# Gathered rows turned by DMA as fp16 halves, instead of by TensorE as fp32, in an attention and mixture-of-experts kernel

## The chip, the cores and the metric

The kernel runs on one core of one Trainium2 chip. The metric is the device time of one execution in microseconds (us); a run is timed several times and the median counts. A separate execution, recorded by the hardware profiler, gives the profile and the trace. Engines are named as in the profile: PE is TensorE's matmul, PEld its weight load, DVE VectorE, ACT ScalarE, POOL GpSimd, SP SyncE, and SPq the DMA queue that SP issues.

## The reference

Thresholded attention makes 4608 rows `x` of 512 numbers. Each row goes to one of 8 experts, which is a two-layer network with a ReLU, and comes back scaled by its gate.

```python
x = attn_out.transpose(0, 2, 1, 3).reshape(B * S, H * D)       # 4608 x 512
e_idx = np.argmax(x @ w_gate, axis=1)
for e in range(8):
    mask = e_idx == e
    h = np.maximum(x[mask] @ w1[e], 0.0)                       # 512 -> 1024
    out[mask] = gate_w[mask, None] * eom[mask, e, None] * (h @ w2[e])
```

## The kernel before

The first part, to about 464 us of the trace, is attention. Its rows are scattered by expert into a DRAM buffer `xs`. The second part runs the experts over **units**, blocks of rows of one expert that lie together in `xs`. There are 12, numbered 0 to 11, of 366, 424, 496, 420, 256, 512, 256, 504, 256, 396, 256 and 496 rows. The first two have a size and place fixed ahead, the third a fixed place; the rest are picked at run time (`choose`, a chain of small DVE operations). A unit of 256 rows is narrow (two tiles of 128 rows), the others are wide (four tiles, unit 0 three).

`Experts.run` walks the units in eight **columns** each (`f` = 0 to 7, 128 of the 1024 hidden features at a time). In a column PE runs `first(f)` (12 matmuls of f16 over all rows of the unit: the operands are split into a high and a low f16 part, `xh`, `xl`, `w1h`, `w1l`), ACT makes the ReLU `hr` and its high part `hh`, DVE the low part `hl`, and PE runs `second` of the column two back. In between the loop places other work: half a weight chunk split into f16 (`split_until`: ACT makes `w1h` or `w2h`, DVE `w1l` or `w2l`), the largest value of a later chunk (`look`), one step of the router (`advance`, `aside`), loads of weights (`load_next`, tile `r`) and of rows (`gather_next`, tiles `xg` wide and `xgn` narrow). The order on PE, DVE, ACT and POOL is the order of this code; SP's order is the framework's.

The rows arrive with a row on each partition. The matmuls want features on partitions, so each unit's rows are prepared while the unit before runs:

1. `level` hands out the pieces of `even`: the largest absolute value of each row (`most`, L933, two tiles at a time), a power of two from it (`xup`), then the rows scaled in place (`scale`: L943 on DVE, or L941 on ACT for units 1 to 4).
2. `prep` in columns 5 and 6 (6 and 7 of unit 1): PE turns the scaled fp32 rows against an identity into PSUM (`px`, L1260; L1397 in class `Turned`, the units of 424, 420 and 396 rows), ACT casts `xh` out of PSUM (L984), DVE subtracts for `xl` (L990).

Unit 0 does the same inside the attention's last steps. Class `Turned` also loads its rows in three DMAs so that its short tile comes first.

Of the kernel before, what the change touches and what calls it, by code (L numbers as in the profile page):

```python
# [430 lines left out]
class Router:  # L431
# [5 lines left out]
    def __init__(self, ctx, tc, ntok, E, DM, sizes, cut):  # L437
# [260 lines left out]
    def choose(self):  # L698
# [14 lines left out]
        for k, z in enumerate(self.SLOTS):  # L713
            yield
            read = z if z < self.TURNED else -(-z // P) * P
            V.scalar_tensor_tensor(key[:, 0:E], st[:, 1], float(read), st[:, 0], op0=ALU.is_ge, op1=ALU.mult)
            V.tensor_reduce(top, key, axis=AX.X, op=ALU.max)
            V.tensor_scalar(cand, key[:, 0:E], top, None, op0=ALU.is_equal)
            V.tensor_tensor(pick, st[:, 2:4], cand[:, None, :].broadcast_to([1, 2, E]), op=ALU.mult)
            yield  # L720
            V.tensor_reduce(got, pick, axis=AX.X, op=ALU.add)
            V.tensor_scalar(self.prows[:, 1, k : k + 1], got[:, 0:1], -1.0, dummy, op0=ALU.mult, op1=ALU.add)
            V.tensor_copy(self.prows[:, 0, k : k + 1], got[:, 1:2])
            V.scalar_tensor_tensor(
                st[:, 0:3], cand[:, None, :].broadcast_to([1, 3, E]), -float(z), st[:, 0:3], op0=ALU.mult, op1=ALU.add
            )
            self.tables.append(k)
# [69 lines left out]
class Experts:  # L797
# [28 lines left out]
    def open(self):  # L826
# [7 lines left out]
        ]  # L834
        self.xp = self.pool("ex", 2)
        self.fp = self.pool("ef", 1)
# [90 lines left out]

    def even(self, xg, other=False):
# [3 lines left out]
        def most(a, b):  # L932
# [5 lines left out]
        def scale(a, b):  # L938
            for t in range(a, b):
                if other:  # L940
                    self.nc.scalar.activation(xg[:, t, 0:DM], xg[:, t, 0:DM], AF.Copy, scale=up[:, t : t + 1])  # L941
                else:
                    V.tensor_scalar(xg[:, t, 0:DM], xg[:, t, 0:DM], up[:, t : t + 1], None, op0=ALU.mult)  # L943

        two = [(t, min(t + 2, n)) for t in range(0, n, 2)]
        return down, [lambda f=f, ab=ab: f(*ab) for f in (most, scale) for ab in two]

# [103 lines left out]

    def level(self, i, k):
        for n in sorted(self.since):
            if self.column - self.since[n] >= self.LOOK and (n < i + 3 or i > 3) or n == i + 1 and k >= -4:
                del self.since[n]
                self.pieces += [(n, x) for x in self.unit(n).even()]
        if i == 1 and k < -1:
            return
        self.pieces.sort(key=lambda x: x[0])
        due = sum(n == i + 1 for n, _ in self.pieces)  # L1060
        assert not due or k < 0
        count = max(int(self.unit(i).N > 2 * P), due + 1 + k if due else 0)
        for _ in range(min(count, len(self.pieces))):
            self.pieces.pop(0)[1]()

# [74 lines left out]
    def run(self):  # L1140
# [4 lines left out]
        for i in range(nun):  # L1145
            b, final = self.unit(i), i == nun - 1
            late = i == rt.early - 1
            for f in range(8):
# [25 lines left out]
                self.look(i, f)  # L1174
                self.level(i, k)
                for _ in range(1 if self.padded else 6 if rt.last else 3 if i or f else 0):
# [34 lines left out]
class Base:  # L1211
# [22 lines left out]
    def even(self):  # L1234
        self.down, pieces = self.ex.even(self.xg[:, 0 : self.nt], 0 < self.i < 5)
        return pieces

# [3 lines left out]

    def prep(self, k, later=None):
        ex, nc, rt, nt = self.ex, self.nc, self.ex.rt, self.nt
        if k == 1 and later is None:
            self.key()
        if k == 0:
            n = 512 if ex.units[0] is not self else nt * P
            self.xh = ex.xp.tile([P, 4, n], F16, name="xh")
            self.xl = ex.xp.tile([P, 4, n], F16, name="xl")
        chunks = 4 if nt == 2 else 2  # L1250
        if k * chunks >= 4:
            return
        pts = ex.px()
        hs = [slice(0, 64), slice(64, P)]
        for c in range(chunks):
            cs = slice((chunks * k + c) * P, (chunks * k + c + 1) * P)
# [4 lines left out]
        at = lambda x: x[:, chunks * k : chunks * k + chunks, 0 : nt * P].rearrange("p c (t h j) -> p h c t j", h=2, j=64)  # L1261

        def out():
            for h in range(2):
                pts[h] = pts[h][:, 0 : chunks * nt * 64].rearrange("p (c t j) -> p c t j", t=nt, j=64)
# [4 lines left out]
        if later is None:  # L1270
            out()
        else:
            later.append(out)

# [61 lines left out]
class Pair(Base):  # L1336
# [9 lines left out]
    def load(self, dst, r0, n):  # L1346
        rt = self.ex.rt
        src = rt.xs[bass.ds(self.row + r0, n), :]
        ins = self.nc.sync.dma_start(dst, src if n < P else src.rearrange("(t p) w -> p t w", p=P))
        rt.after(ins, [x for _, x in rt.tok])  # L1350
        rt.after(ins, rt.pads)

    def gather(self):
        self.xg = self.ex.rows_tile(self.nt)
        self.load(self.xg[:, 0 : self.nt], 0, self.nt * P)


# [18 lines left out]
class Turned(Pair):  # L1376
    def gather(self):
        xg = self.xg = self.ex.rows_tile(self.nt)
        m = self.nt - 1
        self.z = self.N - m * P  # L1380
        self.load(xg[:, 1 : self.nt], self.z, m * P)
        for pp in (slice(0, 64), slice(64, P)):
            self.load(xg[pp, 0], 0, 64)

    def prep(self, k):
        ex, nc, xg, m = self.ex, self.nc, self.xg, self.nt - 1
        if k == 1:
            self.key()
        if k == 0:
            self.xh, self.xl = (ex.xp.tile([P, 4, 512], F16, name=n) for n in ("xh", "xl"))  # L1390
        pts = ex.px()
        hs = [slice(0, 64), slice(64, P)]
        for b in range(2 * m + 1):
            for h in range(2):
                c, t = (b // m, 1 + b % m) if b < 2 * m else (h, 0)
                src = xg[hs[h], t, (2 * k + c) * P : (2 * k + c) * P + P]
                nc.tensor.transpose(pts[h][:, b * 64 : b * 64 + 64], src, ex.ident[hs[h], hs[h]])  # L1397
        at = lambda x: x[:, 2 * k : 2 * k + 2, self.z : self.N].rearrange("p c (t h j) -> p h c t j", h=2, j=64)
        parts = []
        for h, pt in enumerate(pts):  # L1400
            src = pt[:, 0 : 2 * m * 64].rearrange("p (c t j) -> p c t j", t=m, j=64)
            parts.append((at(self.xh)[:, h], at(self.xl)[:, h], src))
            one = (x[:, 2 * k + h, 0 : self.z] for x in (self.xh, self.xl))
            parts.append((*one, pt[:, 2 * m * 64 : 2 * m * 64 + self.z]))
        for hi, _, src in parts:
            ex.high(hi, src)
        for hi, lo, src in parts:
            ex.low(lo, src, hi)

    def second(self, f):  # L1410
# [20 lines left out]
    def flip(self, k):  # L1431
        ex, nc = self.ex, self.nc
        for i, pt in enumerate(ex.px()):
            t = 2 * k + i
            o = self.z + (t - 1) * P if t else 0
            for c in range(4):
                nc.tensor.transpose(pt[:, c * P : c * P + P], self.yt[:, c, o : o + P], ex.ident)
            ex.emit_out(pt, self.keys, t, slice(0, P if t else self.z))


class EarlyTurned(Turned):
# [7 lines left out]
    def load(self, dst, r0, n):  # L1449
        rt = self.ex.rt  # L1450
        src = rt.xs[self.row + r0 : self.row + r0 + n, :]
        ins = self.nc.sync.dma_start(dst, src if n < P else src.rearrange("(t p) w -> p t w", p=P))
        rt.read_early(ins)
# [72 lines left out]
def build(tc, qkv, tau, wg, w1, w2, out, shape):  # L1526
    nc = tc.nc
    with ExitStack() as ctx:
# [6 lines left out]
        with tc.manual_schedule(engines=ENGINES):  # L1535
            with ExitStack() as actx:
# [22 lines left out]

                def even():  # L1560
                    for piece in ex.unit(0).even():
                        piece()

                def begin():
# [16 lines left out]

                hooks[end] = even
                hooks[end + 1] = begin
# [55 lines left out]
```

## Time and profile before

| what | value |
|---|---|
| median of 3 timed runs | 888.5 us (887.51 to 890.45) |
| the profiled execution | 884.38 us, with a span of 882.7 us from first to last instruction |
| mean granted TensorE clock in the profiled execution | 0.998 of full speed |
| PE, DVE, ACT busy share of the span | 98%, 87%, 79% |

The span is what the trace shows; 1.7 us of the profiled execution's time lie around it. Time stamps below are in us from the span's start. A busy PE is an engine with matmuls in its pipeline, so the spacing of successive starts tells more than the busy share.

### The profile page before, as it was taken

How to read it: one execution, taken by the hardware profiler on the slowest of the kernel's cores; microseconds unless marked ns; L12 is line 12 of the kernel's file. 1: busy time of each engine (PE TensorE's matmuls, PEld its weight loads, DVE VectorE, ACT ScalarE, POOL GpSimd, SP SyncE). 2: the span in 40 equal slices, each digit the busy share in tenths (PEclk: the TensorE clock that was granted, in tenths of full speed). 3: DMA queues.
4: the chain of work that ended last, by engine and by line, in shares of the span. 5: the costliest groups of instructions: out<-in, count | busy, mean ns of one | idle time of the engine just before them, and what ended most of it. 6: DMA issues, size and time to landing. Idle time of an engine off the chain costs nothing. (4 is left out here: it accounts for less than half of the span.)

```text
span 882.7 us, 22316 instructions
## 1 busy us (share of the span) xinstructions
PE 866.9 (98%) x8271; PEld 524.6 (59%) x8271; DVE 764.8 (87%) x1839; ACT 700.6 (79%) x1349; POOL 407.5 (46%) x692
## 2 busy tenths in 40 slices
PE   8999999999999999999999999999999999999996
PEld 4666666666666666666665544455744655656643
DVE  6999999999999999999998877798797897886631
ACT  6999999998999998998987848776775775786731
POOL 4456656675867658676854650118210310310211
PEclk9999999999999999999999999999999999999999
DMA  6699995223332123313228688455573663550101
GB/s 196 192 273 301 338 308 185 89 92 100 125 104 74 60 80 124 125 45 112 80 84 272 217 257 286 138 159 169 194 233 97 215 214 97 191 190 2 38 24 46
DMA packets 74912, 135.16 MB, mean 153 GB/s; under 512 B 7295, under 2 KB 34175, under 8 KB 74802
## 3 DMA queue, kind: packets, MB, share of 16 engines
q1 hardware_dynamic: 68257, 114.80, 41.8%
q0 software_dynamic: 6544, 18.92, 5.6%
q8 instruction: 66, 1.08, 0.5%
q14 instruction: 45, 0.36, 0.1%
HBM read 95.26 MB, written 40.60 MB: 154 GB/s over the span
## 5 line engine op out<-in xcount | busy, mean ns | idle before, releaser
L177 ACT ACTIVATE p<-s,mn 128x576 f32<-128x576 f32 x288 | 216.0, 800 | 25.6 <-DVE s L159 25.4
L189 DVE SCALAR_TENSOR_TENSOR p<-s,thr,p 128x576 f32<-128x576 f32 x288 | 226.7, 824 | 0.3
L159 DVE TENSOR_SCALAR_CACHE_REDUCE s<-ps 128x576 f32<-128x576 f32 x288 | 206.2, 751 | 13.6 <-PE ps L145 11.4
L145 PE MATMUL ps<-qk 64*128 64x288 f32 (+1 forms) x1280 | 182.7, 419 | 0.0
L974 POOL DMA_INDIRECT out_dram<-yo,kid x39 | 49.4, 1267 | 264.3 <-DVE yo L973 206.9
L166 POOL TENSOR_SCALAR thr<-mn,tau_sb 128x2 f32<-128x2 f32 x144 | 101.7, 706 | 130.1 <-DVE s L159 127.2
L1284 PE MATMUL ph<-xh,w1h 128*128 128x256 f16 (+7 forms) x380 | 124.3, 328 | 0.0
L1284 PE MATMUL ph<-xh,w1l 128*128 128x256 f16 (+7 forms) x380 | 123.9, 327 | 0.0
L1284 PE MATMUL ph<-xl,w1h 128*128 128x256 f16 (+7 forms) x380 | 122.5, 327 | 0.0
L145 PEld LDWEIGHTS ps<-qk 64*128 64x128 f32 (+1 forms) x1280 | 108.2, 178 | 18.3 <-DVE s L159 3.0
L990 DVE TENSOR_TENSOR hl<-hr,hh 128x256 f16<-128x256 f32 (+7 forms) x95 | 53.7, 565 | 63.5 <-ACT hh L984 63.1
L1286 ACT ACTIVATE hr<-ph 128x256 f32<-128x256 f32 (+7 forms) x95 | 46.5, 490 | 78.0 <-PE ph L1284 77.6
L258 PE MATMUL pr<-PTb,vld 128*64 128x320 f32 (+1 forms) x640 | 107.2, 447 | 0.0
L1284 PEld LDWEIGHTS <-w1h 128*128 128x128 f16 x768 | 73.4, 98 | 53.5 <-issue 0.5
L244 PE MATMUL pt<-ident,p 64*128 64x64 f32 x2288 | 95.6, 223 | 0.2
L258 PE MATMUL pa<-PTa,vld 128*64 128x256 f32 (+1 forms) x640 | 84.6, 391 | 0.3 <-ACT PTb L218 0.3
L244 PEld LDWEIGHTS pt<-ident,p 64*128 64x128 f32 x2288 | 83.1, 139 | 0.8 <-ACT PTa L247 0.4
L1306 PE MATMUL py<-w2h,hh 128*128 128x512 f16 (+3 forms) x213 | 80.8, 380 | 0.0
L1307 PE MATMUL py<-w2l,hh 128*128 128x512 f16 (+3 forms) x213 | 80.7, 379 | 0.0
L247 ACT COPY PTa<-pt 128x1024 f32<-128x1024 f32 x64 | 67.5, 1054 | 0.0
L324 POOL TENSOR_TENSOR rows<-xl,rinv 128x256 f32<-128x256 f32 x64 | 61.4, 960 | 10.7 <-ACT xl L369 10.4
L247 ACT COPY PTb<-pt 128x1024 f32<-128x1024 f32 x63 | 65.4, 1038 | 0.0
(249 smaller groups left out, 1679.9 us busy)
## 6 DMA issues: line engine op xcount, KB each, us to landing
r<-in_moe_w_dram SPq DMA_DIRECT2D x104, 512.0 KB, 5.4
xs<-zrow SPq DMA_DIRECT2D x74, 257.0 KB, 7.8
qk<-in_qkv_dram SPq DMA_DIRECT2D x31, 608.0 KB, 4.1
vld<-in_qkv_dram SPq DMA_DIRECT2D x32, 320.0 KB, 5.8
xg<-xs SPq DMA_DIRECT2D x4, 1028.0 KB, 5.9
xg<-xs SPq DMA_DIRECT2D x4, 771.0 KB, 4.7
xgn<-xs SPq DMA_DIRECT2D x4, 514.0 KB, 4.6
xg<-xs SPq DMA_DIRECT2D x6, 128.5 KB, 6.9
```

The lines of the kernel that those rows point to most:

```text
L145: nc.tensor.matmul(ps[a][rows, o : o + HS], q[pp, t * P : t * P + w], k[pp, k0 : k0 + HS], start=True, stop=True)
L159: nc.vector.tensor_scalar(s, ps[a][:, c0 : c0 + S], SC, None, op0=ALU.mult, op1=ALU.min, accum_out=mn[:, a : a + 1])
L166: self.router.gate = nc.gpsimd.tensor_scalar(thr, mn, self.tau, None, op0=ALU.add)
L177: self.nc.scalar.activation(e, ss[a], AF.Exp, bias=mn[:, a : a + 1], scale=-1.0)
L189: nc.vector.scalar_tensor_tensor(e, s, thr[:, a : a + 1], e, op0=ALU.is_le, op1=ALU.mult, accum_out=acc[:, a ^ (t > 1) : (a ^ (t > 1)) + 1])
L244: nc.tensor.transpose(pt[:, o : o + 64], p[hs[h], k0 : k0 + P], id_[hs[h], hs[h]])
L247: nc.scalar.copy(d, pt.rearrange("p (h b j) -> p b h j", h=2, j=64))
L258: one = lambda out, l, r, start, stop: nc.tensor.matmul(out, l, r, start=start, stop=stop, skip_group_check=True)
L324: nc.gpsimd.tensor_tensor(o, xl[:, a, 0:4, 0:D], ra[:, a, 0:4, None].broadcast_to([P, 4, D]), op=ALU.mult)
L1284: nc.tensor.matmul(ph, w[:, c, fs], x[:, c, 0:N], start=(i == 0), stop=(i == 11))
L1306: nc.tensor.matmul(Y, hh[:, ts], wh, start=(f == 0), stop=False)
L1307: nc.tensor.matmul(Y, hh[:, ts], wl, start=False, stop=False)
```

## The change

All units but unit 0 stop using PE for the turn. `most` stays. The scaling in place goes, and so do `prep`'s turns and PSUM reads. In their place a piece `turn(t)` for each tile of 128 rows makes both halves with rows still on partitions, into one tile `xb` (128 x 1024 f16: ACT writes `xb`'s high half scaled by `xup`, DVE its low half), and SP issues one DMA transpose that writes the 8 blocks of 128 x 128 straight into `x`, which holds `xh` and `xl` together. `level` hands out `most` pieces of any unit ahead but `turn` pieces of the next unit alone, spread so that they are through by column 4 (column 5 for unit 2, whose pieces start in column 4 of unit 1). `key()` (the output scales) stays in column 6. Class `Turned` loads its rows like the other units, short tile last, so that it reads four whole tiles; `xs` gets 128 rows more, and one more DMA of zeros fills them. `choose` now asks for whole tiles of rows for every slot. From the reference's inputs the experts get 619, 496, 677, 491, 670, 499, 508 and 648 rows, with which both forms of the rule pick the same experts and leave no rows over.

```diff
-        self.xs = dram.tile([self.A + sum(self.base.values()), self.W], F32, name="xs")
+        self.xs = dram.tile([self.A + sum(self.base.values()) + P, self.W], F32, name="xs")
...
-            read = z if z < self.TURNED else -(-z // P) * P
+            read = -(-z // P) * P
...
+    def turn(self, x, xg, up, t):
+        both = self.halves_of_rows.tile([P, 2, 512], F16, name="xb")
+        src, up = xg[:, t, 0 : self.rt.DM], up[:, t : t + 1]
+        self.high(both[:, 0], src, up)
+        self.low(both[:, 1], src, both[:, 0], up)
+        self.nc.sync.dma_start_transpose(x[:, :, t * P : t * P + P], both.rearrange("p a d -> p (a d)"))
...
-    def level(self, i, k):
+    def level(self, i, f):
+        end = 5 + (i == 1)
         for n in sorted(self.since):
-            if self.column - self.since[n] >= self.LOOK and (n < i + 3 or i > 3) or n == i + 1 and k >= -4:
+            if self.column - self.since[n] >= self.LOOK and (n < i + 3 or i > 3) or n == i + 1 and f > 0:
                 del self.since[n]
-                self.pieces += [(n, x) for x in self.unit(n).even()]
-        if i == 1 and k < -1:
+                most, turn = self.unit(n).even()
+                self.pieces += [(n, 0, x) for x in most] + [(n, 1, x) for x in turn]
+        if i == 1 and f < 4:
             return
         self.pieces.sort(key=lambda x: x[0])
-        due = sum(n == i + 1 for n, _ in self.pieces)
-        assert not due or k < 0
-        count = max(int(self.unit(i).N > 2 * P), due + 1 + k if due else 0)
-        for _ in range(min(count, len(self.pieces))):
-            self.pieces.pop(0)[1]()
+        due = sum(n == i + 1 for n, _, _ in self.pieces)
+        assert not due or f < end
+        count = max(int(self.unit(i).N > 2 * P), -(-due // (end - f)) if due else 0)
+        for _ in range(count):
+            may = [x for x in self.pieces if x[0] == i + 1 or not x[1]]
+            if may:
+                self.pieces.remove(may[0])
+                may[0][2]()
...
-                k = f - (6 if late else 5)
-                if not final and k in (0, 1):
-                    self.unit(i + 1).prep(k)
+                if not final and f == 6:
+                    self.unit(i + 1).key()
```

Three places of the order that the change gives, each before and after. On PE, the end of unit 1 and the start of unit 2 (496 rows), before:

```order
L1423 LDWEIGHTS w2h
L1423 MATMUL py<-hl,w2h 128x424
L1260 MATMUL px<-ident,xg 128x64 x16
L1284 LDWEIGHTS w1h
L1284 MATMUL ph<-xh,w1h 128x496
```

and after, where the line numbers are those of the changed file:

```order
L1398 LDWEIGHTS w2h
L1398 MATMUL py<-hl,w2h 128x424
L1281 LDWEIGHTS w1h
L1281 MATMUL ph<-x,w1h 128x496
```

The 16 turns in front of the unit's first matmul are gone, and that matmul now reads `x`, which a DMA writes.

On DVE, columns 5 and 6 of unit 1, where unit 2's rows are prepared, before:

```order
L990 TENSOR_TENSOR hl<-hr,hh 128x424
L992 SCALAR_TENSOR_TENSOR w2l<-r_8582,up,w2h 128x1024
L933 TENSOR_REDUCE ax<-xg 128x2 x2
L935 TENSOR_SCALAR ax<-ax 128x4
L891 TENSOR_SCALAR xup<-ax 128x4
L892 TENSOR_SCALAR xdown<-ax 128x4
L716 SCALAR_TENSOR_TENSOR key<-st 1x8
L717 TENSOR_REDUCE top<-key 1x1
L718 TENSOR_SCALAR cand<-key,top 1x8
L719 TENSOR_TENSOR pick<-st,cand 1x16
L990 TENSOR_TENSOR hl<-hr,hh 128x424
L990 TENSOR_TENSOR xl<-px,xh 128x8x64 x2
```

and after, columns 4 and 5 of the same unit:

```order
L933 TENSOR_REDUCE ax<-xg 128x2 x2
L935 TENSOR_SCALAR ax<-ax 128x4
L891 TENSOR_SCALAR xup<-ax 128x4
L892 TENSOR_SCALAR xdown<-ax 128x4
L991 SCALAR_TENSOR_TENSOR xb<-xg,xup,xb 128x512
L721 TENSOR_REDUCE got<-pick 1x2
L722 TENSOR_SCALAR picks<-got 1x1
L723 CAST picks<-got 1x1
L724 SCALAR_TENSOR_TENSOR st<-cand,st 1x24
L989 TENSOR_TENSOR hl<-hr,hh 128x424
L991 SCALAR_TENSOR_TENSOR w2l<-r_8584,up,w2h 128x1024
L991 SCALAR_TENSOR_TENSOR xb<-xg,xup,xb 128x512 x3
```

The two reductions and the first low half moved one column earlier; the other three low halves stand behind column 5's weight split.

On SP, the same stretch of unit 1, before (`r1` and `r2` are weight tiles, `picks` the table that names later units):

```order
L860 DMA r1_9487<-in_moe_w1_dram 128x4x256
L860 ISA
L860 DMA r2_9488<-in_moe_w2_dram 128x2x512
L1332 TENSOR_LOAD picks_154
L1332 ISA x2
L1333 TENSOR_LOAD picks_154
L1333 ISA x2
L860 ISA
L860 DMA r1_9524<-in_moe_w1_dram 128x4x256
```

and after:

```order
L860 DMA r1_9417<-in_moe_w1_dram 128x4x256
L945 DMA_TRANSPOSE x_9240<-xb_9241 128x8x128
L1329 TENSOR_LOAD picks_154
L1329 ISA x2
L1330 TENSOR_LOAD picks_154
L1330 ISA x2
L860 ISA
L860 DMA r2_9418<-in_moe_w2_dram 128x2x512
L945 DMA_TRANSPOSE x_9240<-xb_9286 128x8x128
L945 DMA_TRANSPOSE x_9240<-xb_9290 128x8x128
L945 DMA_TRANSPOSE x_9240<-xb_9294 128x8x128
```

Unit 2's four transposes stand in the one queue among the weight loads: one after column 4's loads, three together after column 5's.

## Rows read from the trace of the kernel before

**Rows 1.** Page, part 1: busy us (share of span), instructions.

```profile
PE 866.9 (98%) x8271; PEld 524.6 (59%) x8271; DVE 764.8 (87%) x1839; ACT 700.6 (79%) x1349; POOL 407.5 (46%) x692
```

**Rows 2.** Busy time by stretch of the experts' part; columns in the first line.

```profile
core 0: us, PE busy (x) PEld busy (x) DVE busy (x) ACT busy (x) POOL busy (x), PEclk, DMA share, GB/s
...
520.00:540.00 20.00, 18.95 (x125) 10.20 (x124) 14.46 (x34) 13.49 (x21) 2.31 (x3) 1.00 0.96 297
...
620.00:645.00 25.00, 25.00 (x196) 17.00 (x195) 20.94 (x32) 20.68 (x37) 6.19 (x5) 1.00 0.63 203
```

**Rows 3.** PE in time near 637: start, us, line, operation, count.

```profile
636.28 0.38 PE L1307 MATMUL py<-w2l,hh 128*128 128x512 f16 x1
...
636.93 0.59 PE L1309 MATMUL py<-w2h,hl 128*128 128x512 f16 x2
637.46 0.71 PE L1260 MATMUL px<-ident,xg 64*128 64x64 f32 x16
638.10 0.28 PE L1284 MATMUL ph<-xh,w1h 128*128 128x256 f16 x1
```

**Rows 4.** PE in time near 570, a group of class Turned.

```profile
569.49 1.03 PE L1309 MATMUL py<-w2h,hl 128*128 128x512 f16 x4
...
571.03 0.38 PE L1284 MATMUL ph<-xh,w1h 128*128 128x496 f16 x1
```

**Rows 5.** PE in time, unit 1's turns and its first matmul.

```profile
486.99 0.81 PE L1309 MATMUL py<-w2h,hl 128*128 128x512 f16 x3
...
489.29 0.33 PE L1284 MATMUL ph<-xh,w1h 128*128 128x366 f16 x1
...
492.45 0.81 PE L1309 MATMUL py<-w2h,hl 128*128 128x512 f16 x3
...
494.47 0.33 PE L1284 MATMUL ph<-xh,w1h 128*128 128x366 f16 x1
...
498.28 0.34 PE L1284 MATMUL ph<-xh,w1h 128*128 128x424 f16 x1
```

**Rows 6.** PE in time, unit 2's turns and its first matmul.

```profile
529.30 0.88 PE L1423 MATMUL py<-hl,w2h 128*128 128x424 f16 x4
...
532.52 0.35 PE L1284 MATMUL ph<-xh,w1h 128*128 128x424 f16 x1
...
536.11 0.88 PE L1423 MATMUL py<-hl,w2h 128*128 128x424 f16 x4
...
537.56 0.38 PE L1284 MATMUL ph<-xh,w1h 128*128 128x496 f16 x1
```

**Rows 7.** Groups by line, 464 to 877: busy us, mean ns.

```profile
L992 DVE SCALAR_TENSOR_TENSOR w2l<-r,up,w2h 128x1024 f16<-128x1024 f32 x40 | 51.3, 1282 | 0.0
...
L986 ACT ACTIVATE w2h<-r,up 128x1024 f16<-128x1024 f32 x40 | 45.9, 1147 | 0.0
...
L941 ACT ACTIVATE xg<-xg,xup 128x512 f32<-128x512 f32 x12 | 7.9, 709 | 4.5 <-issue 3.5 <-DVE xup L891 1.0
L943 DVE TENSOR_SCALAR xg<-xg,xup 128x512 f32<-128x512 f32 x16 | 7.8, 528 | 0.0
```

**Rows 8.** Page, part 5, one row: DVE on 576 columns.

```profile
L189 DVE SCALAR_TENSOR_TENSOR p<-s,thr,p 128x576 f32<-128x576 f32 x288 | 226.7, 824 | 0.3
```

**Rows 9.** DVE in time, where unit 1's and unit 2's last halves would follow.

```profile
489.62 1.21 DVE L886 TENSOR_REDUCE mx<-r 128x1 f32<-128x1024 f32 x1
...
526.62 2.34 DVE L933 TENSOR_REDUCE ax<-xg 128x2 f32<-128x1024 f32 x2
```

**Rows 10.** Weight loads (L860): issue to landing, the whole span.

```profile
DMA to landing us min/median/max: 3.2/5.4/10.8
```

**Rows 11.** The same, for loads issued from 478 to 541.

```profile
DMA to landing us min/median/max: 5.7/8.1/10.8
```

**Rows 12.** PE in time, first matmuls of units 4 and 5.

```profile
618.00 0.27 PE L1284 MATMUL ph<-xh,w1h 128*128 128x256 f16 x1
...
644.06 0.38 PE L1284 MATMUL ph<-xh,w1h 128*128 128x512 f16 x1
```

More of the change, by code (lines that the diff above doesn't have):

```diff
@@ L926, in spread, with largest, some @@
         return out
-    def even(self, xg, other=False):
+    def largest(self, xg):
         V, n, DM = self.nc.vector, xg.shape[1], self.rt.DM
         ax, up, down = (self.kp.tile([P, 4], F32, name=x)[:, 0:n] for x in ("ax", "xup", "xdown"))
-        def most(a, b):
+        def some(a, b):
             V.tensor_reduce(ax[:, a:b], xg[:, a:b, 0:DM], axis=AX.X, op=ALU.max, apply_absolute_value=True)
@@ L936, in most @@
                 self.powers(up, down, ax)
[L938 to L946, printed above, removed]
+        return up, down, [lambda t=t: some(t, min(t + 2, n)) for t in range(0, n, 2)]
+    def turn(self, x, xg, up, t):
[4 more added lines that the diff above has]
+        self.nc.sync.dma_start_transpose(x[:, :, t * P : t * P + P], both.rearrange("p a d -> p (a d)"))
     def rows_tile(self, nt):
@@ L1146, in run @@
             b, final = self.unit(i), i == nun - 1
-            late = i == rt.early - 1
             for f in range(8):
@@ L1234, in even @@
     def even(self):
-        self.down, pieces = self.ex.even(self.xg[:, 0 : self.nt], 0 < self.i < 5)
-        return pieces
+        ex, xg = self.ex, self.xg
+        up, self.down, most = ex.largest(xg[:, 0 : self.nt])
+        for x in most:
+            x()
+        for t in range(self.nt):
+            rows = xg[:, t, 0 : ex.rt.DM]
+            self.nc.vector.tensor_scalar(rows, rows, up[:, t : t + 1], None, op0=ALU.mult)
     def key(self):
@@ L1240, in key, with prep @@
         self.keys = self.ex.keys(self.xg[:, 0 : self.nt], back, self.down)
[L1242 to L1245, printed above, removed]
+    def prep(self, k, later):
+        ex, nc, nt = self.ex, self.nc, self.nt
         if k == 0:
[L1247 to L1252, printed above, removed]
+            self.xh, self.xl = (ex.xp.tile([P, 4, nt * P], F16, name=n) for n in ("xh", "xl"))
         pts = ex.px()
         hs = [slice(0, 64), slice(64, P)]
-        for c in range(chunks):
-            cs = slice((chunks * k + c) * P, (chunks * k + c + 1) * P)
+        for c in range(2):
+            cs = slice((2 * k + c) * P, (2 * k + c + 1) * P)
             for t in range(nt):
@@ L1268, in out @@
                 ex.low(at(self.xl)[:, h], pts[h], at(self.xh)[:, h])
[L1270 to L1273, printed above, removed]
+        later.append(out)
     def first(self, f):
@@ L1355, in gather, with even, turn @@
         self.load(self.xg[:, 0 : self.nt], 0, self.nt * P)
+    def even(self):
+        xg = self.xg[:, 0 : self.nt]
+        up, self.down, most = self.ex.largest(xg)
+        def turn(t):
+            if t == 0:
+                x = self.x = self.ex.xp.tile([P, 8, 512], F16, name="x")
+                self.xh, self.xl = x[:, 0:4], x[:, 4:8]
+            self.ex.turn(self.x, xg, up, t)
+        return most, [lambda t=t: turn(t) for t in range(self.nt)]
 class Fixed(Pair):
@@ L1376 @@
 class Turned(Pair):
[L1377 to L1408, printed above, removed]
     def second(self, f):
@@ L1434, in flip @@
             t = 2 * k + i
-            o = self.z + (t - 1) * P if t else 0
+            pp = self.part(t)
             for c in range(4):
-                nc.tensor.transpose(pt[:, c * P : c * P + P], self.yt[:, c, o : o + P], ex.ident)
-            ex.emit_out(pt, self.keys, t, slice(0, P if t else self.z))
+                nc.tensor.transpose(pt[pp, c * P : c * P + P], self.yt[:, c, t * P :][:, pp], ex.ident)
+            ex.emit_out(pt, self.keys, t, pp)
 class EarlyTurned(Turned):
@@ L1450, in load @@
         rt = self.ex.rt
-        src = rt.xs[self.row + r0 : self.row + r0 + n, :]
-        ins = self.nc.sync.dma_start(dst, src if n < P else src.rearrange("(t p) w -> p t w", p=P))
+        ins = self.nc.sync.dma_start(dst, rt.xs[self.row + r0 : self.row + r0 + n, :].rearrange("(t p) w -> p t w", p=P))
         rt.read_early(ins)
@@ L1558, in prep @@
                     ex.unit(0).prep(k, outs)
-                def even():
-                    for piece in ex.unit(0).even():
-                        piece()
                 def begin():
@@ L1580, in first @@
                     ex.unit(0).first(0)
-                hooks[end] = even
+                hooks[end] = lambda: ex.unit(0).even()
                 hooks[end + 1] = begin
```

11 lines of the change are left out of this document (5 added, 6 removed).

## The prediction

> **What bounds the kernel now.** I read the busy shares first: PE 98%, DVE 87%, ACT 79% of the span [rows 1]. A busy PE may only be a full pipeline, so the second view is the stretches of the experts' part: from 620 to 645 PE is busy for all 25.00 us at a granted clock of 1.00, DVE for 20.94 and ACT for 20.68; from 520 to 540, early in the part, PE loses about a us and the DMA engines are busy for 0.96 of the time [rows 2]. The third is PE in order of time. Three starts of 512-column matmuls take 0.65 us from 636.28 to 636.93, 0.217 each, one column a cycle at 2.4 GHz [rows 3]. So PE is the bound in the experts' part, and at its peak rate: what is taken off PE comes off the end, one for one, unless PE must then wait. The chain that ended last is of no help, since it breaks off in the final output DMA.
>
> **What PE sheds.** 18 groups of turns go: one for each of the four narrow units, two for each of the seven wide ones after unit 0 (16 or 14 matmuls each, 276 in all). What a group costs is read from the last matmul before it to the first after it, less the normal spacing of what stands before. At 636.93 two matmuls should take 2 x 0.217, to 637.36; the next unit's work starts at 638.10: 0.74 [rows 3]. In class Turned four from 569.49 should end at 570.36, and 571.03 is 0.67 later [rows 4]. Units 3 to 11 have ten groups of the first kind and four of the second: 10 x 0.74 + 4 x 0.67 = 10.1 us.
>
> Units 1 and 2 cost more now because PE waits within the turns for rows being scaled. Unit 1: 486.99 + 3 x 0.217 = 487.64, continued at 489.29, so 1.65; 492.45 + 0.65 = 493.10, continued at 494.47, so 1.37 [rows 5]. Unit 2: matmuls of 424 columns take 424/512 of 0.217, 0.18; 529.30 + 0.72 = 530.02, continued at 532.52, so 2.50; 536.11 + 0.72 = 536.83, continued at 537.56, so 0.73 [rows 6]. Together 6.25, and with 10.1 the most that can be won from PE is 16.4 us.
>
> **What ACT and DVE exchange.** ACT's cast out of PSUM becomes a scaled write of 512 columns from SBUF: between half of 1.147 and the 0.709 that the scaling of the same 512 columns takes [rows 7]; I take 0.7. DVE's subtraction becomes a three-operand one: 0.824 for 576 columns and 1.282 for 1024 give 1.02 ns a column, so 0.76 for 512 [rows 7, 8]. A wide unit thus gets 4 x 0.76 = 3.0 us of DVE work and loses at least, from unit 5 on, the scaling, 4 x 0.53 = 2.1, besides the old subtractions, which I don't even count [rows 7]. In 620 to 645 DVE has 4.06 us free and ACT 4.32 [rows 2], so the exchange costs nothing; without this cover it is at most 0.9 us in a unit.
>
> **What a DMA transpose costs.** The trace of before has none. Its nearest rows are the weight loads, on the same queue, with twice its 256 KB: issue to landing 3.2 us at least, 5.4 in the median, 10.8 at most [rows 10], and 5.7, 8.1, 10.8 in the busy stretch from 478 to 541 [rows 11]. I bound a transpose by 3.2 and 10.8 and assume that, like the loads, several are under way at once. For units 3 to 11 this is hidden by the rest of the unit before. The tightest case is a wide unit after a narrow one: unit 4 lasts from 618.00 to 644.06, 26 us [rows 12], the four `turn` pieces go out in columns 0 to 3, half of that, and 13 us remain for a last landing of at most 10.8. On SP, the transposes stand among weight loads for a unit or more ahead; these lose a few us of lead, and nobody waits for them.
>
> Unit 1 has less room. Its last `turn` stands on DVE behind the reduction that ends at 489.62 + 1.21 = 490.83 [rows 9]; with 0.76 it ends at 491.6. The queue is emptier by then, so I take the median, 5.4: rows ready at 497.0. PE would be there at 498.28 - 3.02 = 495.3 [rows 5]. So it waits 1.7 and starts 1.3 us ahead of before.
>
> Unit 2 is worse. All its pieces stand in columns 4 and 5 of unit 1. Behind the weight split that makes way at 526.62 [rows 9] come, in the place of the old work, what is left of two reductions (2.34), 0.5 of small ones and four low halves (3.04): 526.62 - 1.3 + 5.9 = 531.2 for the last. Three transposes are then issued together behind weight loads and row loads, in the stretch where the DMA engines are full [rows 2]. With 8.1, the nearest row [rows 11], the rows are ready at 539.3. PE would be there at 537.56 - 1.3 - 3.23 = 533.0 [rows 6]; it waits 6.3 and starts unit 2 1.7 us later than before. All of the 6.25 us of the first two units is lost again, and 1.7 besides. With 3.2 it starts at 534.4, 3.2 ahead; with 10.8 at 542.0, 4.4 behind.
>
> **The sum.** 10.1 - 1.7 = 8.4 us of gain, with bounds of 13.3 and 5.7. The profiled execution took 884.38, so 876.0 for that one; it lies 4.1 below the median of the timed runs. Against the median of 888.5 I predict 880.1, and by the bounds 875 to 883.
>
> The extra DMA of zeros and the 128 rows lie in attention, where SP's queue has room; the reads of whole tiles move more bytes in three units only.
>
> [...] By the spacing above PE turns a block of 128 x 128 (a pair of half turns, eight pairs in 0.64 us from 637.46 to 638.10) in 0.08 us [rows 3]. [...]
>
> **The rivals.**
> *Early units hidden too.* The transposes land near 3.2 us even behind full queues. For it: they are half the size of a load. Against it: loads in that stretch never landed under 5.7 [rows 11]. Gain 13 to 16: 872 to 875.
> *No change.* DVE takes PE's place in the narrow units, where it is busy for 20.94 of 25 us and PE's stretch shrinks by 0.74 to 1.5 [rows 2, 3]. It decides once DVE's added work is over the 4 us free; by the exchange above it is not. Price: the 10.1 us go and the early loss stays partly: 886 to 891.
> *Slower: transposes that go one at a time.* If each holds the queue for its whole time t, the four of a wide unit need 4t. In the four narrow units there are 26 us, less 2 for the first piece. From t = 6.0 on they are late; at t = 6.5 four delays of 4t - 24 = 2 us have eaten the 8.4. At 10.8 [rows 10] each delay is 19 us, and four make 77: 880 + 77 = 957. For it: the loads' times are those of transfers that overlap, which a transpose needn't do. Against it: 10.8 was taken with full queues, and the DMA engines are busy for only 0.63 of 620 to 645 [rows 2]. [...]
>
> **How the numbers follow.** I give 0.62 to the main case (875 to 883), 0.13 to early units hidden, 0.09 to no change, 0.12 to one at a time, and 0.04 to a smaller gain through several short waits. About 0.3%, 2.7 us, is what a measurement of this kernel can tell from no change. Faster: 0.62 + 0.13 + 0.04 = 0.79; same: 0.09; slower: 0.12. The range of 871 to 888 takes in the main case, its better neighbour and most of the one without change; the slow case stays out.
>
> **What would show it.** Right: no turns into `px` after unit 0; PE without a gap at unit starts from unit 3 on; its longest wait of the part ahead of unit 2's first matmul, on a DMA into `x`, some 6 us; transposes that land in 3 to 11 us and overlap. Wrong: PE waiting for `x` at units 5, 7, 9 and 11 (one at a time), or PE waiting for `hl` or weights in narrow units (DVE).

## The result, and the profile after

The changed kernel takes 893.09 us in the median of 4 runs (892.47 to 893.18), the kernel before 888.0 beside it (886.05 to 890.45): a ratio of 1.0054, with an interval of 1.0028 to 1.008. It is slower by half a per cent where I forecast 880.1 and gave slower 0.12. The profiled execution took 893.15 us, with a span of 891.3.

The busy shares first, which answer to [rows 1]:

```profile
PE 857.6 (96%) x7995; PEld 516.7 (58%) x7995; DVE 756.7 (85%) x1805; ACT 697.1 (78%) x1323; POOL 408.3 (46%) x692
```

PE has shed 9.3 us of busy time and DVE 8.1, and still the end is 8.6 us later than in the first trace of before. So PE stands idle where it did not. The stretches answer to [rows 2]:

```profile
core 0: us, PE busy (x) PEld busy (x) DVE busy (x) ACT busy (x) POOL busy (x), PEclk, DMA share, GB/s
464.00:500.00 36.00, 30.11 (x212) 17.03 (x209) 26.84 (x49) 22.88 (x39) 13.21 (x22) 0.97 0.86 242
500.00:520.00 20.00, 19.24 (x90) 9.70 (x89) 19.45 (x52) 15.76 (x24) 15.74 (x15) 0.88 0.72 213
520.00:540.00 20.00, 20.00 (x113) 10.85 (x112) 13.14 (x34) 8.28 (x12) 9.47 (x9) 1.00 0.89 289
540.00:560.00 20.00, 9.32 (x39) 4.00 (x37) 9.22 (x22) 9.05 (x14) 0.00 (x0) 0.74 0.94 270
...
620.00:645.00 25.00, 25.00 (x161) 15.58 (x159) 19.39 (x31) 17.51 (x29) 13.13 (x22) 1.00 0.51 165
```

From 540 to 560 PE is busy for 9.32 us of 20, and the mean granted clock is 0.74; from 620 to 645 it is full again. From 500 to 520 PE is busy, but the clock is 0.88. PE's waits in the experts' part, longest in the last column:

```profile
engine line waited for: us in total, times, longest us
PE ph L1281 <- DMA x<-xb: 11.4, 2, 10.7
PE ph L1281 <- ACT hr L1283: 4.6, 1, 4.6
PE px L903 <- DVE red L898: 2.3, 1, 2.3
```

Two waits for `x`, no more: those of units 1 and 2. PE in order of time, the first matmuls of units 1, 2 (and the pace behind it) and 3:

```profile
506.64 0.52 PE L1281 MATMUL ph<-x,w1h 128*128 128x424 f16 x2 [0.76 <-DMA x<-xb]
...
551.79 0.98 PE L1281 MATMUL ph<-x,w1h 128*128 128x496 f16 x2 [10.68 <-DMA x<-xb]
...
554.63 0.62 PE L1281 MATMUL ph<-x,w1l 128*128 128x496 f16 x1
555.04 0.62 PE L1281 MATMUL ph<-x,w1h 128*128 128x496 f16 x1
...
598.24 0.52 PE L1281 MATMUL ph<-x,w1h 128*128 128x420 f16 x2
```

Behind the 10.68 us of idleness the matmuls of 496 columns start 0.41 us apart, at a granted clock of 0.51 from 551.5 to 556; at the pace of [rows 3] it would be 0.21. This costs PE about 2 us more, until some 555.9. It had been so before, ahead of unit 1, at the wait for `hr`:

```profile
499.23 0.46 PE L1281 MATMUL ph<-xh,w1h 128*128 128x366 f16 x1 [4.59 <-ACT hr L1283]
...
499.79 0.51 PE L1281 MATMUL ph<-xh,w1l 128*128 128x366 f16 x1
500.09 0.51 PE L1281 MATMUL ph<-xh,w1h 128*128 128x366 f16 x1
```

Matmuls of 366 columns start 0.30 us apart there, where the pace of [rows 3] gives 0.155, and so on until some 504.9; from 499 to 505 the granted clock was 0.52. That is about 2.7 us more, so most of unit 1's lateness is the 4.6 us of waiting for `hr` and the slow clock behind it; the wait for `x` itself is 0.76.

Why unit 1 is late stands on ACT and SP. ACT, the last high half of unit 1 and what follows it, and the same of unit 2:

```profile
498.09 0.72 ACT L985 ACTIVATE xb<-xg,xup 128x512 f16<-128x512 f32 x1 [8.60 <-DMA x<-xb]
498.72 0.46 ACT L1283 ACTIVATE hr<-ph 128x366 f32<-128x366 f32 x1
...
547.36 0.72 ACT L985 ACTIVATE xb<-xg,xup 128x512 f16<-128x512 f32 x1 [10.25 <-DMA x<-xb]
```

`xb` has three buffers and a wide unit four tiles. The fourth half needs the first tile's buffer, so it waits until the first transpose has landed (issued at 489.07, done by 498.09, so 9.0 us later; at unit 2 issued at 536.61, done by 547.36, 10.75 later); the ReLU `hr` stands behind it on ACT, and PE behind `hr` (the 4.6 us). SP, which issues loads and transposes in order (start, us of issue):

```profile
467.24 21.73 SPq L860 DMA_DIRECT2D r<-in_moe_w_dram  x14
489.07 7.92 SPq L945 DMA_TRANSPOSE x<-xb  x2
497.08 1.08 SPq L860 DMA_DIRECT2D r<-in_moe_w_dram  x2
498.26 4.88 SPq L945 DMA_TRANSPOSE x<-xb  x2
...
518.07 0.40 SPq L1378 DMA_DIRECT2D xg<-xs  x1
...
536.61 6.00 SPq L945 DMA_TRANSPOSE x<-xb  x1
544.08 0.40 SPq L860 DMA_DIRECT2D r<-in_moe_w_dram  x1
544.57 5.55 SPq L945 DMA_TRANSPOSE x<-xb  x3
```

Fourteen weight loads are issued at the start of unit 0 and occupy SP for 21.7 us, 3.45 at most for one. The first transpose, whose halves DVE has completed by about 486, goes out only at 489.07, and the first two hold SP for 4 us each on average, the first of unit 2 for 6.00. Over all 36:

```profile
L945 SPq DMA_TRANSPOSE x<-xb x36: 1231/1352/6002, 489.1 to 832.8; - x36
```

### The profile page after: what moved, and what is told of

Read it like the earlier page. It is cut to its first block, busy times and chain, and to the rows that moved or that the text cites. A ratio compares the mean times of both kernels' runs of the same rounds, so it can differ in the third digit from the quotient of the medians.

```text
span 891.3 us, 21798 instructions
## 1 busy us (share of the span) xinstructions
PE 857.6 (96%) x7995; PEld 516.7 (58%) x7995; DVE 756.7 (85%) x1805; ACT 697.1 (78%) x1323; POOL 408.3 (46%) x692
## 3 DMA queue, kind: packets, MB, share of 16 engines
q1 hardware_dynamic: 106321, 124.51, 47.7%
## 5 line engine op out<-in xcount | busy, mean ns | idle before, releaser
L1281 PE MATMUL ph<-x,w1h 128*128 128x256 f16 (+6 forms) x704 | 170.9, 330 | 11.9 <-DMA x<-xb 11.4
L1281 PEld LDWEIGHTS <-w1h 128*128 128x128 f16 x768 | 75.3, 99 | 75.2 <-issue 21.0
L1281 PE MATMUL ph<-x,w1l 128*128 128x256 f16 (+6 forms) x352 | 115.9, 330 | 0.0
L258 PEld LDWEIGHTS pa<-PTa,vld 128*64 128x64 f32 (+1 forms) x640 | 38.9, 135 | 42.0 <-issue 14.6
```

Source lines behind the costliest of these rows:

```text
L258: one = lambda out, l, r, start, stop: nc.tensor.matmul(out, l, r, start=start, stop=stop, skip_group_check=True)
L1281: nc.tensor.matmul(ph, w[:, c, fs], x[:, c, 0:N], start=(i == 0), stop=(i == 11))
```

## The experiments

The two faults seen above could each be the cause. **RING**: the three tiles of `xb`. **QUEUE**: the transposes come late out of SP's queue and land late, because weight loads stand ahead of them, and any number of tiles would wait. A third view puts it on the transposes' nature.

The kernels were run in three groups, each beside the kernel before on the same chip. Before took 890.0, 887.25 and 884.4 us there, so only ratios are compared between groups. The starts are those of the units' first matmuls in the traces; "rest" is from unit 3's to the end of the span. The first matmul of unit 0, ahead of any transpose, already falls between 466.92 (e9_behind_ring4) and 468.81 (changed), so 2 us between two starts in this table need not come from an edit.

| kernel | ratio to before (95%) | unit 1 | unit 2 | unit 3 | span | rest |
|---|---|---|---|---|---|---|
| before, first trace | | 498.28 | 537.56 | 581.93 | 882.7 | 300.8 |
| before, second trace (e6) | 1.0004 (0.9986 to 1.0023) | 498.69 | 540.29 | 584.66 | 885.7 | 301.0 |
| changed | 1.0054 (1.0028 to 1.008) | 506.64 | 551.79 | 598.24 | 891.3 | 293.1 |
| e1_ring4 | 1.0053 (1.0032 to 1.0074) | 509.59 | 552.35 | 598.28 | 891.7 | 293.4 |
| e2_by_pe_1_2 | 0.9969 (0.9944 to 0.9994) | 498.75 | 543.19 | 589.32 | 886.9 | 297.6 |
| e2_by_pe_2 | 1.0008 (0.9982 to 1.0033) | 504.99 | 550.03 | 596.16 | 890.7 | 294.5 |
| e4_plain | 0.9994 (0.9978 to 1.0011) | 503.60 | 549.61 | 595.38 | 887.5 | 292.1 |
| e7_hold | 0.9999 (0.999 to 1.0008) | 497.47 | 544.90 | 590.82 | 884.2 | 293.4 |
| e3_gather16 | 1.0023 (1.0004 to 1.0043) | 504.11 | 547.69 | 593.85 | 887.3 | 293.5 |
| e5_act_ring4 | 1.049 (1.0475 to 1.0504) | 507.11 | 554.38 | 607.51 | 930.5 | 323.0 |
| e8_by_pe_2_hold | 0.9962 (0.9951 to 0.9973) | 497.32 | 541.26 | 587.40 | 881.2 | 293.8 |
| e9_behind | 0.9955 (0.9942 to 0.9967) | 496.71 | 540.18 | 586.30 | 879.2 | 292.9 |
| e9_behind_ring4 | 0.9946 (0.993 to 0.9963) | 496.39 | 539.26 | 583.70 | 877.7 | 294.0 |
| e9_behind_ring4_gather | 0.9998 (0.9987 to 1.0009) | 497.61 | 539.50 | 589.00 | 881.9 | 292.9 |

**e1_ring4: a fourth tile.** The one-row buffer of `rest` is taken later, to make room.

```diff
-        self.xp, self.halves_of_rows = self.pool("ex", 2), self.pool("exs", 3)
-        self.fp = self.pool("ef", 1)
+        self.xp, self.halves_of_rows = self.pool("ex", 2), self.pool("exs", 4)
...
-        self.flex = self.pool("ewf", 1)
+        self.flex, self.fp = self.pool("ewf", 1), self.pool("ef", 1)
```

> The changed kernel (893.1 us), with four tiles of halves (xb) instead of three, so that no half of a four-tile unit has to wait for a transpose to land; everything is still computed. Theory RING (the ring of three puts ScalarE behind the landing of the unit's first transpose, and what stands behind it on ScalarE, the relu of the unit before, holds TensorE): ScalarE's two idle stretches before the fourth half, 8.60 us at 498.09 and 10.25 us at 547.36, are gone, TensorE's wait of 4.6 us for hr near 499 goes, its wait of 10.68 us for x at 551.79 shrinks to under 3 us, and the time is 879 to 883 us. Rival QUEUE (the transposes are late in SyncE's own in-order queue, behind weight loads that hold it 3 to 6 us each and behind the gather of unit 3, whatever the ring): ScalarE's waits go but TensorE then waits for x at the starts of units 1 and 2 for nearly as long, and the time is 888 to 893 us.

No gain: 1.0053. PE's waits for `x` of e1, by its rows in order of time:

```profile
509.59 0.86 PE L1280 MATMUL ph<-x,w1h 128*128 128x424 f16 x2 [11.53 <-DMA x<-xb]
...
552.35 0.98 PE L1280 MATMUL ph<-x,w1h 128*128 128x496 f16 x2 [4.17 <-DMA x<-xb]
```

ACT no longer waits for a transpose, and the wait for `hr` is gone too, but PE stands 11.53 us at unit 1 for `x` itself. RING names a wait that is there, but taking it away gains no time while the loads stand ahead: my own first reading of the trace falls, and QUEUE stands. At unit 2 the wait for `x` did shrink, from 10.68 us to 4.17; unit 1 began 3 us later and ate it. Where the expectation says that loads hold SP 3 to 6 us each, the rows show 3.45 at most.

**e2: the old way for units 1 and 2, or unit 2 alone.** `prep` of `Base` comes back for the units in a list, into the new tile `x`, with the rows scaled by ACT and the pieces timed as before. The second kernel's list is (2,).

```diff
+    BY_PE = (1, 2)
...
+                if i + 1 in self.BY_PE and f - 5 - (i == 1) in (0, 1):
+                    self.unit(i + 1).prep(f - 5 - (i == 1))
```

> The changed kernel with units 1 and 2 alone turned by TensorE as before (rows scaled in place by ScalarE, sixteen turns in each of two columns, halves out of PSUM), units 3 to 11 by DMA; everything is still computed. RING and QUEUE alike (all of the loss lies at units 1 and 2; from unit 3 on the change gains 8.2 us, by the first matmuls of unit 3 and the span's end): 888.0 - 8.2 = 880 us, 878 to 882, unit 3 begins within 2 us of before's 581.93. Rival TRAFFIC (the 36 transposes, six times the small packets, slow the other transfers all along, attention's end 1.6 us later included): 884 us or more, with unit 3 still begun over 4 us late.

> The changed kernel with unit 2 alone turned by TensorE as before; unit 1 and units 3 to 11 by DMA; everything is still computed. It splits the loss: by the first matmuls, unit 1 begins 8.3 us late (1.6 of them from attention) and unit 2's part is 16.3 - 8.3 = 8.0 us. RING and QUEUE, if the two units' losses are each their own: 893.1 - 8.0 = 885 us, 883 to 887, with unit 1 begun at about 506 as in the changed kernel. If instead the first loss brings the second (the pieces of unit 2 are late because the gathers behind unit 1's transposes are), unit 2 by TensorE starts late as well: 888 us or more.

With both units by PE the kernel is faster than before, 0.9969, and 0.85% under the changed kernel: that much hung on eight of the 36 transposes. It is less than the 0.9% below before that I expected; its runs spread from 882.7 to 891.1, the profiled one (888.71) is among the long ones, and its units 2 and 3 begin 3 and 5 us after those of the second trace of before. What makes its long executions long I did not follow.

With unit 2 alone by PE hardly anything is won at unit 2 in the trace, where it begins at 550.03: the second way of the expectation. (By the ratios this kernel is 0.46% under the changed one, with wide intervals; the profiled execution, 892.43, is above its median of 890.94.) Its rows are gathered late, SP's row for that gather:

```profile
516.40 0.48 SPq L1397 DMA_DIRECT2D xg<-xs  x1
```

In e2_by_pe_1_2 the same gather goes out at 509.41. Between these two traces unit 1 begins 6.2 us and unit 2 6.8 us apart, so unit 1's lateness brings most of unit 2's.

**e4_plain: copies instead of transposes.**

```diff
-        self.nc.sync.dma_start_transpose(x[:, :, t * P : t * P + P], both.rearrange("p a d -> p (a d)"))
+        self.nc.sync.dma_start(x[:, :, t * P : t * P + P], both.rearrange("p a (c d) -> p (a c) d", d=P))
```

> The changed kernel with each of the 36 transposes replaced by a plain copy of the same bytes between the same tiles, from the same place in the same queue, so that x holds untransposed blocks and the experts' outputs are not those of the reference. QUEUE (the place in the queue and the full rings make the lateness): the copies hold SyncE and land as late as the transposes, 889 to 894 us. Rival NATURE (a transposing transfer is itself slow and dear, about 1.45 us of all 16 engines each, and holds the queue longer than a copy): copies land in a few us, ScalarE's waits shrink below 4 us each, and the time is 883 to 887 us.

By the ratios the transposing costs 0.6%, some 5 us, which puts the copies between the two expectations (0.9994 of 888 is 887.5). With copies PE still waits 10.33 us for `x` at unit 2 and ACT 17.3 us in its two stands (18.8 in the changed kernel). The copies' hold on SP, to set against the transposes' above:

```profile
L945 SPq DMA_DIRECT2D x<-xb x36: 593/606/3890, 486.9 to 829.6; - x36
```

Less than half as long in the median, and still 3.89 us at the worst. NATURE is a part, and not the one that makes the stall at unit 2. The expectation's 1.45 us for each transpose is an estimate from two pages: SP's queue took 41.8% of 16 engines' span before and 47.7% after, and 5.9% of 891.3 us over 36 transposes is 1.46. That rings are full, as some expectations have it, no view here shows; the rows give the time that an issue held SP.

**e6_before: the kernel before again.**

> The kernel before, once more, unchanged: its profiled execution took 884.38 us while its runs take 886 to 893. If the starts of units 1 to 4 (498.28, 537.56, 581.93, 618.00) are its usual ones and the rest is spread over the span, they come again within 1 us. If one of them moves by 2 us or more, the difference between the two traces at that unit is partly the spread of the kernel before, and the loss of the change is smaller there than a comparison with the first trace says.

PE, the first matmuls of its units 2 and 3:

```profile
540.29 0.38 PE L1284 MATMUL ph<-xh,w1h 128*128 128x496 f16 x1
...
584.66 0.34 PE L1284 MATMUL ph<-xh,w1h 128*128 128x420 f16 x1
```

Unit 2 begins 2.7 us later than in [rows 6], and all that follows with it. So 2.7 of the 14.2 us by which unit 2 of the changed kernel lags the first trace are the spread of the kernel before. Against the second trace the account closes: 7.95 us lost by unit 1's start, 11.5 by unit 2's, 13.6 by unit 3's, then 8.0 won back, 5.6 at the end.

**e7_hold: unit 1's loads held back.**

```diff
-        while self.nload < min(len(self.seq), self.nsplit + self.ahead, n + max(0, self.column - n + 2)):
+        most = n + max(0, self.column - n + 2) if self.column > 4 else n - 6
+        while self.nload < min(len(self.seq), self.nsplit + self.ahead, most):
```

> The changed kernel with four of the fourteen weight loads that unit 0's first column issues held back until column 5, behind unit 1's four transposes; everything is still computed. e1 left QUEUE: TensorE waits for x at units 1 and 2 with three tiles of halves or four. QUEUE, unit 1: T0 is issued at 485 to 486 (when its halves are ready) instead of 489.07, holds SyncE about 1.3 us instead of 4.58 because the rings have room, lands in 3 to 5 us, so the fourth half runs before 491 and unit 1 begins at 498 to 500 instead of 506.64; unit 2 stays as late against its own rows as it is (its wait is in its own stretch), so 893.1 - 5 = 888 us, 886 to 890. Rival LATENCY (a transpose that stands in any queue takes some 9 us, loads or none): unit 1 begins at 504 or later and the time is 892 to 894 us. Third way: the loads held back are missed by the measuring of unit 2's weights (TensorE waits for red), and the time is above 893 us.

SP of e7, unit 1:

```profile
484.72 4.32 SPq L945 DMA_TRANSPOSE x<-xb  x2
489.10 0.57 SPq L860 DMA_DIRECT2D r<-in_moe_w_dram  x1
489.77 1.25 SPq L945 DMA_TRANSPOSE x<-xb  x1
491.07 0.58 SPq L860 DMA_DIRECT2D r<-in_moe_w_dram  x1
493.06 1.24 SPq L945 DMA_TRANSPOSE x<-xb  x1
```

With ten loads ahead instead of fourteen unit 1 begins at 497.47, earlier than in either trace of before, and the kernel gains 0.55%. That the loads ahead make unit 1 late is confirmed, and LATENCY, as it is put here, is not: the fourth tile's transpose went out at 493.06, and the unit began 4.4 us later. PE still waits 7.52 us for `x` at unit 2.

The third way of the expectation came too, in part. The loads held back arrive late for the measuring of unit 2's weights: three reductions stand together on DVE, and PE waits for what follows them.

```profile
511.82 3.45 DVE L886 TENSOR_REDUCE mx<-r 128x1 f32<-128x1024 f32 x3
```

```profile
515.87 0.27 PE L903 MATMUL px<-ident,red 128*2 128x128 f32 x1 [3.60 <-DVE got L721]
```

At this place PE waits 0.60 us in the first trace of before and not at all in the changed kernel. The same 3.6 us stand in e9_behind and e9_behind_ring4, so the gains of e7 and e9 are what is left after this price.

**e3_gather16: unit 3's gather held back.**

```diff
+                    if n > rt.early and self.column < 16:
+                        break
```

> The changed kernel with the gathers of units 3 and later held back until unit 2 has begun, so that SyncE, in order, does not stand at unit 3's gather waiting for the padding writes while unit 2's transposes come up behind it; everything is still computed. QUEUE, unit 2: the wait of SyncE at the gather (6.73 us to 529.7) goes, the weight loads and unit 2's transposes move up by up to that much, and PE's wait of 10.68 us at 551.79 shrinks to 4 to 7 us: 887 to 890 us. Rival (unit 2's lateness is made at unit 1 and in SyncE's weight loads, which wait for their buffers, not for the gather): no change of unit 2's start against unit 1's (551.8 - 506.6 = 45.2 us), 892 to 894 us; if unit 3's rows come late for it, more.

About half of what was expected of it: 0.3% less than the changed kernel, with unit 2's wait at 7.61 us instead of 10.68. Of the 4.1 us by which its trace begins unit 2 earlier, 2.5 are there at unit 1, before the edit can act.

**e5_act_ring4: transposes from ScalarE's queue.** Four tiles, and `self.nc.sync.dma_start_transpose` becomes `self.nc.scalar.dma_start_transpose`.

> The changed kernel with four tiles of halves and with all 36 transposes issued from ScalarE's queue instead of SyncE's, so that none stands behind a weight load's issue; the engines that move the bytes stay the same, and everything is still computed. QUEUE (issue order and full rings of SyncE's queue make x late): unit 1 begins by 500, unit 2's wait for x falls below 3 us, and, since ScalarE now stands 36 times for the low half and the issue (1.2 us and up each), some of it is given back: 880 to 886 us. LATENCY (the bytes take that long in engines that the weight loads fill): units 1 and 2 begin at 504 to 507 and 549 to 552 as now, and with ScalarE's stands on top the time is 893 to 900 us.

Far slower. ACT's waits of e5, the experts' part:

```profile
ACT hr L1282 <- issue: 39.7, 16, 2.9
...
ACT xb L984 <- issue: 12.3, 3, 4.7
```

ACT stands 52 us for issuing, PE 25.7 us for `hr`, and the rest after unit 3 grows from 293 to 323 us. Unit 2 waits 10.52 us for `x` as before, but as ACT is late itself, its start does not tell whether a queue of its own would bring `x` sooner. The packets at unit 1 do. ACT's rows, then the DMA queues from 484.9 to 489, 489 to 494 and 494 to 498 (packets, MB, share of 16 engines); q1 is SP's queue, q10 the transposes', 1056 packets each:

```profile
484.91 1.36 ACTq L944 DMA_TRANSPOSE x<-xb  x1
...
487.85 3.77 ACTq L944 DMA_TRANSPOSE x<-xb  x1
```

```profile
q1 hardware_dynamic: 1171, 1.48, 105.5%
...
q1 hardware_dynamic: 905, 1.19, 88.4%
q10 hardware_dynamic: 822, 0.21, 25.1%
...
q10 hardware_dynamic: 1290, 0.31, 89.9%
q1 hardware_dynamic: 301, 0.47, 33.5%
```

No load stands in this queue, and still nothing of the first transpose is moved in the 4 us to 489, while SP's loads fill the DMA engines. By 494 it is not through, 9 us after its issue, as in the changed kernel (489.07 to 498.09); the second one's issue holds ACT 3.77 us. So at unit 1 a queue of its own does not help: the loads that the DMA engines still have to move are enough to make `x` late, wherever it is issued. Here LATENCY, as e5's expectation has it, holds. With ten loads ahead, in e7, the fourth half's wait for the first tile ends at 490.23, 5.5 us after the issue at 484.72.

**e8 and e9: what is left at unit 2.** e8 joins e7 and unit 2 by PE. e9 puts the loads of columns 12 to 15 behind unit 2's last transpose; its second form adds e1's fourth tile, its third also e3's edit.

```diff
-            ins = nc.sync.dma_start(r, s.rearrange("(c p) f -> p c f", p=P))
+            with self.tc.issue_after(self.turned) if self.column in (12, 13, 14, 15) else ExitStack():
+                ins = nc.sync.dma_start(r, s.rearrange("(c p) f -> p c f", p=P))
```

> The loads held back as in e7 (unit 1 begun at 497.5, 886.9 us), and unit 2 alone turned by TensorE; everything is still computed. In e7 unit 3 begins at 590.9 against 584.75 in the second trace of the kernel before, and from there to the end it takes 293.3 us against 301.0. QUEUE (what is left of the loss lies at unit 2's own transposes): unit 2 begins at 539 to 541, unit 3 at 584 to 586, and the time is 886.9 - 6 = 881 us, 879 to 883. Rival (what starts TensorE early at unit 1 is given back by VectorE and ScalarE before unit 3, by the waits for red and for scaled rows): unit 3 begins at 588 or later and the time is 884 us or more.

> As e7, and the weight loads of columns 12 to 15 are put behind unit 2's fourth transpose in SyncE's order, so that none of unit 2's transposes stands behind a load that waits for its buffer (in e7 T0 went out at 531.52 and T1 to T3 at 537.24 to 542, with halves ready at 530.9 and 534.3); three tiles of halves, all still computed. QUEUE: T1 and T2 go out by 536, the fourth half runs by 537 instead of 540.48, unit 2 begins at 541 to 542 instead of 545.0: 883 to 885 us. Rival RING (with three tiles the fourth half still waits for T0's landing, 7 us here, whatever the order of the queue): unit 2 begins at 544 or later, 886 to 888 us. If the loads come late for it, unit 3 pays and the time is above 888.

> As e9_behind with four tiles of halves. In e1 the fourth tile gained nothing because the transposes were late in the queue; with the queue cleared the two add up if both bind. RING and QUEUE together: the fourth half at 535, all four transposes out by 539, unit 2 begun at 540 to 541.5, 881 to 884 us, 1 to 3 us less than e9_behind. QUEUE alone: within 1 us of e9_behind.

> As e9_behind_ring4, with the gathers of units 3 and later held back until unit 2 has begun (e3 alone made 890.6 of 893.1 us). If SyncE's stand at unit 3's gather (for the padding writes) is what delays unit 2's transposes once the loads are out of the way: 1 to 3 us less than e9_behind_ring4, 879 to 882 us, T0 out before 531. If unit 2's rows (gathered at 512, after the scatter of rows) and its column in the program set T0: no change within 1 us, or later units pay for late rows.

e8 is faster than before by 0.4%, with unit 3 begun at 587.40, between its two theories. e9_behind turns by DMA throughout and does as well: 0.45% under before. The fourth tile's further 0.09% is within the intervals. Of e9_behind_ring4, the last low halves of units 1 and 2 on DVE, SP, and PE's first matmul of unit 2:

```profile
491.20 0.74 DVE L992 SCALAR_TENSOR_TENSOR xb<-xg,xup,xb 128x512 f16<-128x512 f32 x1
...
532.89 2.06 DVE L992 SCALAR_TENSOR_TENSOR xb<-xg,xup,xb 128x512 f16<-128x512 f32 x3
```

```profile
530.89 6.75 SPq L945 DMA_TRANSPOSE x<-xb  x4
537.85 2.85 SPq L860 DMA_DIRECT2D r<-in_moe_w_dram  x4
```

```profile
539.26 0.58 PE L1283 MATMUL ph<-x,w1h 128*128 128x496 f16 x2 [1.90 <-DMA x<-xb]
```

Four transposes in a row, and the unit begins 8.4 us after the first was issued. This version is the fastest tried, by its median. Holding the gathers back as well loses all of it: unit 2 begins as early, but unit 3 only 49.5 us later (44.4 in e9_behind_ring4). Of these 5.1 us, 1.7 are a longer wait of PE for `red`, the largest weights of unit 3 (4.0 us for 2.3). Most of the rest is the clock, granted at 0.85 from 540 to 550 and 0.83 from 560 to 570, where e9_behind_ring4 has 1.00, some 1.5 and 1.7 us.

## Why the prediction was wrong

**PE as the bound, and what it sheds: right.** 512 columns in 0.217 us [rows 3] are 2.36 columns a ns: that is the prediction's 2.4 GHz, with one column a cycle assumed; the trace itself gives the clock as a share of full speed, 1.00 there. PE does not wait for `x` from unit 3 on. Of 10.1 us for units 3 to 11, 1.3 belong to unit 3's own two groups and lie before its start; of the other 8.8 the changed kernel won 8.0 against the second trace of before, 7.7 against the first. Unit 3's 1.3 were not won: unit 2 lasts 46.45 us instead of 44.37, with about 2 us of the low clock and 2.3 us for `red` in it (0.8 before).

**The exchange on ACT and DVE: right.** A high half took 707 ns, a low half 752 in the median; I had 0.7 and 0.76. No engine but PE became the bound in the narrow units.

**The transposes of units 1 and 2: the step that failed.** I wrote that for unit 1 "the queue is emptier by then, so I take the median", and priced each transpose from issue to landing only. I had not asked when SP could issue it, nor what the DMA engines would still have to move. Fourteen loads were ahead; the first transpose went out at 489.07 and was done by 498.09, 9.0 us where the sum has 5.4; the last held SP until 503.1, and unit 1 began at 506.64 instead of 497.0. Unit 2 was to begin 1.7 us later than before and began 14.2 later (11.5 by the second trace), because the delay of unit 1 carries over and the same happens again. With the loads out of the way, in e9_behind_ring4, the two units begin at 496.39 and 539.26, against 497.0 and 539.3 in the prediction. For unit 1 this is the forecast's own path: last half at 491.9 (forecast 491.6), begun 4.5 us later (forecast 5.4). For unit 2 the agreement is luck: the last half came at 534.95, not 531.2, and the unit began 4.3 us later, not 8.1; two errors cancel. What had no term in the sum is the work ahead of a transpose, in SP's queue and in the DMA engines.

**What I did not see at all.** That three tiles serve four, which stops ACT (real, but e1 shows that it costs nothing while the queue is the limit); and that PE's granted clock was 0.52 and 0.51 after waits of 4.6 and 10.7 us. My signs of being right came all the same (no turns, no gap at unit starts from unit 3 on, the longest wait for `x` ahead of unit 2): they looked at the units where the prediction held, and put 6 us on a wait that was 10.7.

**The rivals.** "No change" did not come: from unit 3 on PE waits for neither `hl` nor weights in the narrow units. My slower rival, transposes one at a time, gives the right sign by the wrong mechanism: it needed 6 us a transpose in the narrow units, where nothing waits. Four took 8.4 us from first issue to use in e9_behind_ring4, 2.1 each at most.

**Open:** how much of e7's and e9's gain is SP free to issue and how much the DMA engines with less work ahead. Both change together there; e5 shows for unit 1 that the engines' work alone is enough, and for unit 2 it does not tell. And 0.54% is all that the best version gained: its unit 2 begins 1.7 us after the first trace of before, and its rest is 6.8 us shorter, not 8.8.

## What to carry to other kernels

When work moves from a compute engine to a DMA, price four things: when its queue can issue it (here at 489.07, with the halves complete by about 486), how long the issue holds the queue (1.35 us in the median, 6.00 at most), what the DMA engines still have to move ahead of it (in e5 nothing of the first transpose was moved in the 4 us to 489), and the landing (9.0 us after the issue at unit 1, 5.5 in e7). The first is read from the issuing engine's rows, at the places with the least slack. Loads that nobody needs yet are to go behind a transfer that someone waits for; in e5 another queue did not take it past them, and in e7 loads held too long made PE wait 3.60 us elsewhere. A wait seen in a trace, like ACT's 8.60 us for a buffer, may only be the first of two in line: e1 took it away and PE's 11.53 us for `x` took its place.

## What the runs showed that I had not expected

- A transpose of 128 x 1024 f16 held SP for 1.35 us in the median and up to 6.00 us; a copy of the same bytes 0.61, up to 3.89. Issued from ACT it held that engine for 1.27 us in the median, up to 3.84 with no load in its queue, and the kernel went from 1.0054 to 1.049 of before.
- After 10.68 us of idleness PE's granted clock was 0.51 (551.5 to 556): 0.41 us instead of 0.21 between matmuls of 496 columns, for about 4 us. After 4.59 us it was 0.52 (499 to 505): 0.30 instead of 0.155 for 366 columns, for about 5.5 us.
- Executions of one kernel can differ by 2.7 us in where unit 2 begins, and all later work is shifted by it: a single trace is not the kernel.
